# Value loads moved to SP, the activation table loaded first, two weight tiles among the query loads

## Chip, cores and metric

The kernel runs on one core of a Trainium2 chip. The metric is the device time of one execution in microseconds (us). TensorE (PE) multiplies matrices, VectorE (DVE), ScalarE (ACT) and GpSimd (POOL) do elementwise work, SyncE (SP) issues DMAs; ACT can issue DMAs as well.

## What is computed

Attention over 4 batches, 8 heads, 768 positions and head size 64, with a local band (positions closer than 16) joined to 24 block summaries, then layer norm and a two-layer network with a residual:

```python
k_sum = k.reshape(B, H, nb, block, D).max(axis=3)
v_sum = v.reshape(B, H, nb, block, D).mean(axis=3)
scores_l = where(|i - j| < 16, scale * q @ k.T, -1e9)
scores_s = scale * q @ k_sum.T + log(block)
a = softmax(concatenate([scores_l, scores_s]))
attn = a @ concatenate([v, v_sum])
x = heads side by side: (B, S, 512)
xn = (x - mean) / sqrt(var + 1e-6) * g_ln
out = x + maximum(xn @ w_ch1, 0) @ w_ch2        # 512 -> 2048 -> 512
```

The two weight matrices are float64 in memory; the kernel decodes them by integer operations.

## The kernel before

The 3,072 rows are 24 tiles of 128; each tile has two attention steps t of four heads. The first twelve steps (t below 12, the first batch) take an early path in float32: `early_k` copies a window of keys and the block maxima into `kx` (ACT and POOL), `early_qk` multiplies it with the queries `qw` (PE, tile `s`), `softmax` adds the mask and takes the row extreme (DVE, tile `p`) and the exponential (ACT), `early_transp` turns `p` (PE, tile `pp`; ACT copies it to `pT`), `early_pv` multiplies with the values `vw` and with the tail tiles `vst` and `tail` (PE, tile `o`). The block maxima come from four DVE reductions (`kmax`). The block means of the values come from fourteen PE products in `batch_v0` (tile `v`), which need all of the first batch's values; ACT then copies them into the three tail tiles. So no `early_pv` runs ahead of the last value load.

Beside it the weights arrive: `fetch_w(m)` loads a tile of 512 KB (`raw`), `dec_w(m)` decodes it by three DVE instructions and one ACT square, `scale_w` and `conv_w` make two float16 parts of it (`wp`) on ACT and DVE. With them the network's products `g1` (tile `h`) and `g2` (tile `a`) begin; later pairs of tiles use a product scheme of seven multiplications (`sp1`, tiles `qx`, `qy`, `qz`). `warm` gives PE 36 transposes at the start, `spare` is a transpose that fills gaps which the planner foresees on PE.

The order of the work is not written by hand. Every step is recorded by `Plan`, with a cost for each instruction (`cost`, tables `ISSUE`, `LAND`, `SETUP`, `FIRST`), and a list scheduler (`schedule`, called from `search`) makes one list per engine with starting times; `issue` emits the instructions in that order, and each engine runs its list in order. `LOADS` fixes the order of the first loads on SP by hand (`in_front`), ahead of all that the scheduler ranks; `BESIDE` names loads that ACT issues (`queue`): the second half of each of six value tiles. The six calls of `fetch_v0` for a whole tile issue two DMAs of 128 KB each, the seventh one DMA (`vend`, 64 KB). A key tile is 384 KB, a query tile 256 KB, a tail tile two DMAs of 32 KB. Costs of DMAs in the plan: time to issue, bytes by 360 per ns, and a time to landing by kind of step.

Of the kernel before, what the change touches and what calls it, by code (L numbers as in the profile page):

```python
# [18 lines left out]
AF = mybir.ActivationFunctionType  # L19
# [40 lines left out]
RAWS += [f"ring{m}" for m in range(4)]  # L60
AWAY = 24
FILL_IN, FILL_END = 500, 800
LOADS = [("fetch_k0", 0), ("fetch_k0", 1), ("fetch_q", 0), ("gain",), ("fetch_blocks",), ("fetch_k0", 2), ("fetch_k0", 3)]
LOADS += [("fetch_v0", c) for c in range(7)] + [("fetch_tail", 0), ("fetch_q", 1), ("fetch_tail", 1), ("fetch_tail", 2)]
BESIDE = [("fetch_v0", c, 1) for c in range(6)]
NV = 3
HOMES = dict(
    ksg=("qke", "k0_1", "qw4"),
# [30 lines left out]
def in_front(stage, engine):  # L99


    key = (stage[0], *stage[1][:1])
    return LOADS.index(key) if engine == "sync" and key in LOADS else None


class Plan:
# [3 lines left out]
    ENGINES = ("tensor", "vector", "scalar", "gpsimd", "sync")  # L110
    WAIT = dict(tensor=200, vector=140, scalar=160, gpsimd=90, sync=1000)
    SAME = dict(tensor=0, vector=127, scalar=143, gpsimd=100, sync=0)
    SETUP, TICK, SWITCH, FIRST = 1100, 10240 / 3, 93, 3500
    ISSUE = dict(transp=1550, lnT=1250, batch_vput=760, load_q=500)
    LAND = dict(fetch_v0=2050, fetch_k0=1950, fetch_q=2000, fetch_w=1750, fetch_tail=2000, gain=2000)
    LAND |= dict(batch_q=1350, batch_v=1300, load_q=1350, load_v=1150, transp=1050)

    def __init__(self):
# [89 lines left out]
    def cost(self, engine, op, a, k, ins, outs):  # L208

        free = lambda x: math.prod(n for _, n in x.ap[1:])  # L210
        n = max(free(x) for x in ins + outs) if engine != "tensor" else free(a[0])
        if op[:3] == "dma":
            x = (outs + ins)[0]
            return self.ISSUE.get(self.names[self.stage][0], 380 + 70 * (engine == "scalar")), x.ap[0][1] * free(x) * mybir.dt.size(x.dtype) / (200.0 if "transpose" in op else 360.0)
        if engine == "tensor":
            dt = ins[-1].dtype
            if dt == F32R:
                return 0.443 * max(n, 256) + 4.5, 0.0
            if dt == F16 or op == "transpose":
                return max((2 if dt == F32 else 1) * n / 2.4 + 3.0, 28.0), 0.0  # L220
            return max(2 * n / 2.4 + 2.0, 100.0) * 2 if ins[0].ap[0][1] > D else 2 * n / 2.4 + 53.0, 0.0
        psum = any(x.space == bass.MemoryType.PSUM for x in ins)
        pointers = sum(1 for x in ins[1:] if free(x) == 1)
        if engine == "scalar":
            extra = ("accum_out" in k) + sum(isinstance(k.get(x), bass.AP) for x in ("scale", "bias"))
            weights = self.names[self.stage][0] in ("dec_w", "conv_w")
            return n / 1.2 + (51 if psum else 93) + 93 * extra + 35 * weights, 0.0
        if engine == "vector":
            fixed = {"tensor_tensor_reduce": 78, "reciprocal": 90}.get(op, 70) + 61 * pointers
            fixed += 119 * (bool(ins) and self.box(ins[0])[1] == D)  # L230
            return n / (1.92 if op == "tensor_scalar" and not psum else 0.96) + fixed, 0.0
        if op == "tensor_scalar":
            return 180 + n + 61 * pointers + 90 * (n == 1), 0.0
        if op == "tensor_copy":
            return 60 + 3.33 * n, 0.0
        if op == "tensor_tensor":
            shifted = outs[0].offset // outs[0].ap[0][0] != ins[0].offset // ins[0].ap[0][0]
            return 517 if n == 1 else 40 + 2.1 * n + 110 * (shifted or outs[0].dtype == F32R), 0.0
        return 60 + 0.8 * n, 0.0
# [9 lines left out]
    def waits(self, x, real_only=False):  # L249
        wait = []  # L250
        for j, real in x.after.items():
# [3 lines left out]
            else:  # L255
                n = self.names[y.stage][0]
                wait.append((j, (0.0 if real_only else self.slack(x, y)) + (self.LAND.get(n, 1000) if y.dma else self.WAIT[y.engine])))
        return wait
# [157 lines left out]
    def issue(self, nc):  # L416
        for x in self.ops:
            x.first = in_front(self.names[x.stage], x.engine)
        self.watch()
        after = [self.waits(x) for x in self.ops]  # L420
        then = [[] for _ in after]
        for i, x in enumerate(after):
            for j, wait in x:
                then[j].append((i, wait))
        rank = [0.0] * len(after)
        for i in reversed(range(len(after))):
            x = self.ops[i]
            rank[i] = min((rank[j] for j, _ in then[i]), default=0.0) - x.busy - x.moving - self.WAIT[x.engine]
        best = self.search(rank, after, then)
        self.time, self.start, self.end, fills = best  # L430
        for _, i in sorted([*zip(best[1], range(len(after))), *((t, -1) for t in fills)]):
            if i < 0:
                op, a, k = self.ops[self.opens].calls[0]
                getattr(nc.tensor, op)(*a, **k)
                continue
            for op, a, k in self.ops[i].calls:
                getattr(getattr(nc, self.ops[i].engine), op)(*a, **k)  # L437
# [4 lines left out]
def body(ctx: ExitStack, tc, qt, qa, qe, kt, ks, va, vb, vs, g_ln, w1, w2, blocks, out):  # L442
    pl = Plan()
# [8 lines left out]
    def psum(tag, name, shape, at=None):  # L452
        if at is None:
            at = banks[tag] = 1 - banks[tag]
        return pl.tile(pools[tag], shape, F32, f"{tag}{at}", name)
# [12 lines left out]
    wacc = cp.tile([P, 2 * NF], F32, name="wacc")  # L468
# [3 lines left out]
    nc = pl  # L472
# [17 lines left out]
    @pl.step  # L490
    def masks():

        no, far = NEG / QSCALE, nc.gpsimd
        m = msk[:, 1]
        far.memset(m, 0.0)
        for base, a in ((0, 1), (2 * WIN - 2, -1)):
            far.affine_select(m, m, [[a, NC]], compare_op=ALU.is_ge, fill=no, base=base, channel_multiplier=-a)
        far.memset(m[:, P + BLK :], float(np.float32(math.log(BLK)) / np.float32(QSCALE)))
        for t in (0, 2):
            far.tensor_copy(msk[:, t], m)  # L500
        far.memset(msk[:, 0, : WIN - 1], no)
        far.memset(msk[:, 2, P + WIN - 1 : P + BLK], no)

        far.memset(emask[:, :, :D], no)
        far.tensor_copy(emask[:, :, D:], msk[:, :, :P])
        far.tensor_copy(emask[:, :, : NC - P], msk[:, :, P:])
# [28 lines left out]
    def queue(*key):  # L535
        return nc.scalar if any(key[: len(x)] == x for x in BESIDE) else nc.sync

# [103 lines left out]
    @pl.step  # L641
    def batch_s(b):

        mx = work("vm0", f"vm0_{b}", [P, 3])
        nc.vector.tensor_reduce(mx[:], bt["a", b][:], axis=AX.X, op=ALU.max)
        ps = psum("s", f"vps{b}", [P, 512])
        nc.tensor.transpose(ps[:3, :P], mx[:], ident[:])
        m1 = work("vm1", f"vm1_{b}", [3, 8])
        nc.vector.tensor_reduce(m1[:, 0:1], ps[:3, :P], axis=AX.X, op=ALU.max)
        nc.vector.tensor_scalar(m1[:, 0:1], m1[:, 0:1], 2.0**-30, None, ALU.max)  # L650
        mi = m1.bitcast(U32)
        nc.vector.tensor_scalar(mi[:, 1:2], mi[:, 0:1], 0x7F800000, 0x7F800000, ALU.bitwise_and, ALU.bitwise_and)
        nc.vector.tensor_scalar(mi[:, 0:1], mi[:, 1:2], 0x7F800000, 0x7F800000, ALU.bitwise_and, ALU.bitwise_xor)
        nc.vector.tensor_scalar(m1[:, 2:5], ident[:3, :3], m1[:, 0:1], 2.0**13, ALU.mult, ALU.mult)
        nc.vector.tensor_scalar(m1[:, 5:8], ident[:3, :3], m1[:, 1:2], 2.0**-14, ALU.mult, ALU.mult)
        nc.tensor.matmul(ps[:, 128:134], ones[:3], m1[:, 2:8], start=True, stop=True)
        sv = work("sv", f"sv{b}", [P, 10], F32, 2)
        nc.vector.tensor_copy(sv[:, :6], ps[:, 128:134])
        nc.vector.tensor_scalar(sv[:, 6:7], sv[:, 4:5], sv[:, 5:6], QSCALE, ALU.mult, ALU.mult)
        nc.vector.tensor_scalar(sv[:, 7:8], sv[:, 6:7], -1.0, None, ALU.mult)  # L660
        nc.vector.tensor_scalar(sv[:, 8:9], sv[:, 1:2], sv[:, 2:3], None, ALU.mult)
        bt["s", b], bt["c", b] = sv, (sv[:, 7:8], sv[:, 6:7])
# [570 lines left out]
        nc.scalar.activation(gcol[:, 1], gcol[:, 0], AF.Copy, scale=SQ)  # L1233

    @pl.step
    def warm():

        ps = psum("h", "warm", [P, 512])
        with pl.unit():
            for i in range(WARM):  # L1240
                nc.tensor.transpose(ps[:, i % 4 * P : i % 4 * P + P], ident[:], ident[:])
# [40 lines left out]
    def batch(b):  # L1282
# [5 lines left out]
            batch_v(b, c)  # L1288
        batch_s(b)

    warm()
    masks()
    clear()
# [118 lines left out]
```

## Time and profile before

| what | us |
|---|---|
| median of three runs | 615.76 (615.63 to 616.48) |
| profiled execution | 614.82 |
| span of the profiled execution, first to last instruction | 613.0 |
| PE busy in the span | 596.3 (97%) |
| DVE busy in the span | 493.4 (80%) |
| ACT busy in the span | 429.0 (70%) |

Busy time is a mean over stages with different limits, so the views by stretch say more than the table. Instructions of one engine run in the order of its list; idle time before an instruction is put down to what released it last. DMA issues stand in the profile as instructions of the sequencer (SPq, ACTq) and are not counted as busy; nearly every instruction has the line of the planner's emitting loop, so tiles' names tell them apart.

### The profile page before, as it was taken

Reading aid. Unit: us, or ns where it says so; the run is one execution under the profiler, and the core shown is the slowest. Engines: PE = TensorE matmul, PEld = TensorE weight load, DVE = VectorE, ACT = ScalarE, POOL = GpSimd, SP = SyncE. Lnnn points to the kernel's source line nnn. Section 1 sums busy time; section 2 is a strip of 40 time slices with the busy share of each in tenths; the row PEclk is TensorE's granted clock in tenths of the full one; section 3 lists DMA queues with packets and bytes.
Section 4 is the critical chain, followed back from the end, with each engine's and each line's share of the span. In section 5 each row is a group of like instructions: output and inputs, shape, how many; then the busy total and the mean of one; then the engine's idle time right before and its main releaser. Section 6 shows DMA issues by size and latency. Waiting matters only on the chain.

```text
span 613.0 us, 15408 instructions
## 1 busy us (share of the span) xinstructions
PE 596.3 (97%) x5528; PEld 434.0 (71%) x5528; DVE 493.4 (80%) x1260; ACT 429.0 (70%) x1072; POOL 249.0 (41%) x473
## 2 busy tenths in 40 slices
PE   6998899999999999999999999999999999999997
PEld 5586777765677587776866876877777778766675
DVE  3899999999899899999798988889788974633232
ACT  3797798878999977799777857788686575331120
POOL 5122212124675575767664452645445333200000
PEclk9999999999999999999999999999999999999999
DMA  8991388636988977679966757569668461220000
GB/s 250 341 350 31 115 263 279 195 86 138 237 224 203 204 194 181 161 173 220 208 161 150 172 121 152 143 154 198 138 155 180 94 126 45 44 61 18 18 18 35
DMA packets 136237, 95.62 MB, mean 156 GB/s; under 512 B 94561, under 2 KB 118625, under 8 KB 136161
## 3 DMA queue, kind: packets, MB, share of 16 engines
q1 hardware_dynamic: 134528, 93.86, 60.6%
q8 instruction: 43, 0.70, 0.5%
q10 hardware_dynamic: 1632, 0.79, 0.5%
q14 instruction: 34, 0.27, 0.1%
HBM read 66.27 MB, written 6.29 MB: 118 GB/s over the span
## 4 chain that ended last, share of the span: by engine, by line
PE 75%; DVE 13%; DMA 5%; ACT 3%; POOL 2%; issue 1%; SPq 0%; ACTq 0%; POOLq 0%
PE a L437 34%; PE h L437 12%; PE qx L437 10%; PE qz L437 5%; PE s L437 4%; PE o L437 4%; PE qy L437 3%; DVE wf L437 2%; DMA vw<-in_va 1%; DVE raw L437 1%; DVE hl L437 1%; DVE wp L437 1%; PE v L437 1%; DMA ksg<-in_kt 1%; DVE p L437 1%
## 5 line engine op out<-in xcount | busy, mean ns | idle before, releaser
L437 PE MATMUL a<-wp,hh 128*128 128x512 f16 (+1 forms) x768 | 226.6, 377 | 0.0
L437 PEld LDWEIGHTS <-wp 128*128 128x128 f16 x2016 | 163.2, 98 | 25.0 <-issue 2.3
L437 PE MATMUL a<-wp,hl 128*128 128x512 f16 x384 | 144.8, 377 | 0.0
L437 PE MATMUL h<-xs,wp 128*128 128x256 f16 x1152 | 134.1, 273 | 2.2 <-DMA xs<-x 1.0
L437 PEld LDWEIGHTS <-hh 128*128 128x128 f16 x784 | 73.3, 98 | 65.3 <-issue 0.4
L437 POOL TENSOR_TENSOR p<-p,p 128x512 f16<-128x512 f32 x72 | 71.9, 1004 | 35.3 <-ACT p L437 24.5
L437 ACT ACTIVATE p<-p,mn,sv 128x184 f32<-128x184 f32 x144 | 76.1, 530 | 9.1 <-POOL mn L437 8.5
L437 PEld LDWEIGHTS <-hl 128*128 128x128 f16 x392 | 38.3, 98 | 44.6
L437 DVE SCALAR_TENSOR_TENSOR x<-a,wsc,x 128x512 f32<-128x512 f32 (+1 forms) x48 | 35.3, 736 | 22.4 <-PE a L437 22.1
L437 POOL COPY ksg<-ksum 128x48 f32<-128x48 f32 x72 | 29.3, 412 | 52.1 <-DMA ksg<-in_kt 44.8
L437 POOL TENSOR_TENSOR x<-x,rc 128x256 f32<-128x256 f32 x36 | 30.5, 847 | 42.5 <-DVE x L437 31.7
L437 POOL TENSOR_SCALAR mn<-mn,sv 128x2 f32<-128x2 f32 x72 | 31.1, 434 | 40.4 <-DVE mn L437 37.6
L437 DVE CUSTOM_DVE_ANT_0 p<-s,mask 128x184 f32<-128x184 f32 x144 | 42.7, 337 | 3.6 <-PE s L437 3.6
L437 PE MATMUL qx<-xs,wp 128*128 128x128 f16 x576 | 38.4, 219 | 0.0
L437 PEld LDWEIGHTS <-wd 128*128 128x128 f16 x576 | 33.8, 98 | 3.1
L437 DVE SCALAR_TENSOR_TENSOR kl<-ksg,sv,kh 128x368 f16<-128x368 f32 x48 | 34.2, 721 | 1.5 <-ACT kh L437 1.2
L437 ACT ACTIVATE kh<-ksg,sv 128x368 f16<-128x368 f32 x48 | 28.5, 594 | 9.4 <-PE s L437 3.4
L437 DVE SCALAR_TENSOR_TENSOR hl<-h,hh 128x512 f16<-128x512 f32 x48 | 32.3, 678 | 2.0 <-ACT hh L437 1.8
L437 ACT CAST p<-p 128x512 f16<-128x512 f32 x72 | 33.3, 505 | 0.2
L437 ACT ACTIVATE v<-vst,sv 128x512 f16<-128x512 f32 x36 | 25.7, 716 | 9.2 <-PE o L437 7.8
L437 DVE SCALAR_TENSOR_TENSOR v<-vst,sv,v 128x512 f16<-128x512 f32 x36 | 30.2, 838 | 1.3 <-ACT v L437 1.1
L437 ACT ACTIVATE hh<-h 128x512 f16<-128x512 f32 x48 | 28.0, 584 | 4.4 <-PE h L437 4.3
(209 smaller groups left out, 1217.0 us busy)
## 6 DMA issues: line engine op xcount, KB each, us to landing
raw<-in_w SPq DMA_DIRECT2D x32, 512.0 KB
ksg<-in_kt SPq DMA_DIRECT2D x72, 184.0 KB
out_x<-x SPq DMA_DIRECT2D x23, 256.0 KB
qw<-in_qt SPq DMA_DIRECT2D x36, 128.0 KB
vst<-in_va SPq DMA_DIRECT2D x36, 128.0 KB
qs<-in_qt SPq DMA_DIRECT2D x36, 128.0 KB
vst<-in_vb SPq DMA_DIRECT2D x80, 32.0 KB
bst<-in_ks SPq DMA_DIRECT2D x12, 192.0 KB
```

Source lines behind the costliest of these rows:

```text
L437: getattr(getattr(nc, self.ops[i].engine), op)(*a, **k)
```

## The change

Four things change. The second halves of the value tiles, which ACT issued (`BESIDE`), are issued by SP like the first halves. A new step `table`, ranked first on DVE and ACT, clears one column and takes its exponential, so that the activation table is loaded before anything else on ACT. In the fixed order of loads on SP, `gain` (the layer norm's gains, `gcol`) goes from fourth place behind the four key loads, and the first two weight tiles get places of their own: behind the first tail tile, and behind the second. And the costs in the plan are altered: the DMA rings begin at 1300 instead of 3500, the issue of several first loads and of the transposes in `split1` and `split2` is set to its own value, some loads get a rate of their own, weight tiles land after 1550 instead of 1750, `gain` after 3000 instead of 2000.

```diff
-LOADS = [("fetch_k0", 0), ("fetch_k0", 1), ("fetch_q", 0), ("gain",), ("fetch_blocks",), ("fetch_k0", 2), ("fetch_k0", 3)]
-LOADS += [("fetch_v0", c) for c in range(7)] + [("fetch_tail", 0), ("fetch_q", 1), ("fetch_tail", 1), ("fetch_tail", 2)]
-BESIDE = [("fetch_v0", c, 1) for c in range(6)]
+LOADS = [("fetch_k0", 0), ("fetch_k0", 1), ("fetch_q", 0), ("fetch_blocks",), ("fetch_k0", 2), ("fetch_k0", 3), ("gain",)]
+LOADS += [("fetch_v0", c) for c in range(7)] + [("fetch_tail", 0), ("fetch_w", 0), ("fetch_q", 1), ("fetch_tail", 1)]
+LOADS += [("fetch_w", 1), ("fetch_tail", 2)]
+BESIDE = []
...
+    if stage[0] == "table":
+        return 0
...
-    SETUP, TICK, SWITCH, FIRST = 1100, 10240 / 3, 93, 3500
-    ISSUE = dict(transp=1550, lnT=1250, batch_vput=760, load_q=500)
-    LAND = dict(fetch_v0=2050, fetch_k0=1950, fetch_q=2000, fetch_w=1750, fetch_tail=2000, gain=2000)
+    SETUP, TICK, SWITCH, FIRST = 1100, 10240 / 3, 93, 1300
+    ISSUE = dict(transp=1550, lnT=1250, split1=1250, split2=1250, batch_vput=760, load_q=500)
+    ISSUE |= dict(fetch_v0=650, fetch_tail=430, fetch_q=420, fetch_k0=430, gain=430)
+    RATE = dict(fetch_v0=300.0, fetch_w=410.0, fetch_q=385.0)
+    LAND = dict(fetch_v0=2050, fetch_k0=1950, fetch_q=2000, fetch_w=1550, fetch_tail=2000, gain=3000)
...
+    def table():
+        nc.vector.memset(wacc[:, :1], 0.0)
+        nc.scalar.activation(wacc[:, :1], wacc[:, :1], AF.Exp)
...
+    table()
     warm()
```

In `cost`, the bytes of a DMA are divided by the step's `RATE`, where it has one, and by 360 where not.

## Rows read from the trace of the kernel before

**Rows 1.** Busy time by stretch: the stretch and its length in us, busy us and instructions (x) of PE, PE's weight loads, DVE, ACT and POOL, granted share of the TensorE clock, DMA share, GB/s.

```profile
0.00:8.50 8.50, 6.91 (x37) 6.76 (x37) 2.12 (x8) 0.28 (x1) 7.00 (x44) 1.00 0.82 243
8.50:18.90 10.40, 6.84 (x29) 3.63 (x29) 4.03 (x19) 6.29 (x19) 1.60 (x9) 0.84 0.97 296
18.90:80.00 61.10, 55.48 (x450) 45.30 (x449) 58.90 (x182) 51.66 (x143) 12.93 (x36) 1.00 0.60 201
80.00:613.00 533.00, 527.07 (x5017) 378.36 (x5014) 428.32 (x1055) 370.73 (x913) 227.44 (x384) 1.00 0.61 147
```

**Rows 2.** The chain of work that ended last, in order of time, pieces of the first 60 us: start, us, what.

```profile
20.47 3.81 PE v L437 x8
...
40.25 0.69 DVE xs L437
```

**Rows 3.** Busy time of the instructions on the tile `spare` alone (the fillers), by stretch: the stretch and its length, busy us and instructions (x) of PE and of PE's weight loads, granted clock, DMA share, GB/s.

```profile
40.00:60.00 20.00, 5.55 (x46) 5.07 (x46) 1.00 0.35 98
60.00:80.00 20.00, 1.12 (x7) 0.91 (x7) 1.00 0.41 129
```

**Rows 4.** Timeline of DVE up to 19.2 us: start, us, what, and idle time before it with its releaser.

```profile
3.91 0.95 DVE L437 TENSOR_REDUCE kmax<-k 128x24 f32<-128x768 f32 x1 [2.91 <-DMA k<-in_ks]
...
11.01 0.36 DVE L437 CUSTOM_DVE_ANT_0 p<-s,emask 128x192 f32<-128x192 f32 x1 [4.40 <-PE s L437]
...
17.78 0.36 DVE L437 CUSTOM_DVE_ANT_0 p<-s,emask 128x192 f32<-128x192 f32 x1 [3.86 <-PE s L437]
...
18.88 0.42 DVE L437 TENSOR_SCALAR wf<-raw 128x512 uint32<-128x512 uint32 x1
```

**Rows 5.** Timeline of SP's issues up to 20 us: start, us, what.

```profile
0.72 0.87 SPq L437 DMA_DIRECT2D k<-in_ks  x2
1.64 0.64 SPq L437 DMA_DIRECT2D qw<-in_qe  x1
2.32 0.62 SPq L437 DMA_DIRECT2D gcol<-in_g_ln  x1
3.90 0.34 SPq L437 DMA_DIRECT2D blk<-in_blocks  x1
...
8.03 3.94 SPq L437 DMA_DIRECT2D vw<-in_va  x6
...
12.66 0.41 SPq L437 DMA_DIRECT2D qw<-in_qe  x1
```

**Rows 6.** SP's own waits, first from 0 to 13 us and then from 16.5 to 19 us: who waited for what, us in total, times, longest; and the issue that the last of them held.

```profile
SPq L437 <- DMA k<-in_ks: 2.3, 2, 1.4
SPq L437 <- DMA qw<-in_qe: 1.3, 1, 1.3
...
SPq L437 <- DVE mn L437: 0.6, 1, 0.6
SPq L437 <- DMA vw<-in_va: 0.3, 1, 0.3
...
SPq L437 <- DMA raw<-in_w: 0.7, 1, 0.7
...
17.80 0.31 SPq L437 DMA_DIRECT2D tail<-in_vb  x1
```

**Rows 7.** Timeline of ACT up to 10 us.

```profile
0.89 7.25 ACTq L437 DMA_DIRECT2D vw<-in_va  x6
8.22 1.28 ACT L437 ACT_TABLE_LOAD   x1 [8.22 <-DMA vw<-in_va]
9.52 0.52 ACT L437 COPY kx<-k 128x158 f32<-128x158 f32 x2
```

**Rows 8.** Timeline of PE up to 24.3 us.

```profile
8.32 0.27 PE L437 MATMUL s<-ident 128*128 128x128 f32 x1
9.94 0.91 PE L437 MATMUL s<-kx,qw 64*128 64x184 f32 x8 [1.35 <-issue]
...
20.40 2.84 PE L437 MATMUL v<-vw,blk 128*120 128x512 f32 x6
23.17 1.11 PE L437 MATMUL v<-vend,blk 32*120 32x512 f32 x2
```

**Rows 9.** Busy time by stretch as in Rows 1, for three other stretches.

```profile
2.00:8.50 6.50, 6.50 (x37) 6.35 (x35) 1.91 (x2) 0.28 (x1) 5.57 (x34) 1.00 1.04 313
...
13.70:18.90 5.20, 5.17 (x16) 2.54 (x17) 1.34 (x10) 1.98 (x7) 0.70 (x4) 0.67 0.99 312
...
20.00:40.00 20.00, 19.40 (x147) 14.97 (x146) 19.21 (x73) 18.57 (x53) 3.31 (x14) 1.00 1.00 369
```

**Rows 10.** DVE's waits from 18.9 to 80 us: who waited for whom, us in total, times, longest.

```profile
DVE wsc L437 <- POOL wsc L437: 0.7, 1, 0.7
DVE xn L437 <- POOL rs L437: 0.4, 1, 0.4
DVE p L437 <- ACT pT L437: 0.4, 1, 0.4
DVE p L437 <- PE s L437: 0.2, 1, 0.2
```

**Rows 11.** SP's instructions that transpose into the tile `xs` late in the span: count, ns min/median/max, first and last start.

```profile
L437 SPq DMA_TRANSPOSE xs<-x_a x6: 1231/1234/1577, 303.6 to 529.4; - x6
```

**Rows 12.** Timeline of the last microseconds: the last instruction of DVE, with its wait for PE's last.

```profile
609.93 0.48 DVE L437 SCALAR_TENSOR_TENSOR x<-last,wsc,x 128x256 f32<-128x256 f32 x1 [0.17 <-PE last L437]
```

More of the change, by code (lines that the diff above doesn't have):

```diff
@@ L213, in cost @@
             x = (outs + ins)[0]
-            return self.ISSUE.get(self.names[self.stage][0], 380 + 70 * (engine == "scalar")), x.ap[0][1] * free(x) * mybir.dt.size(x.dtype) / (200.0 if "transpose" in op else 360.0)
+            return self.ISSUE.get(self.names[self.stage][0], 380 + 70 * (engine == "scalar")), x.ap[0][1] * free(x) * mybir.dt.size(x.dtype) / (200.0 if "transpose" in op else self.RATE.get(self.names[self.stage][0], 360.0))
         if engine == "tensor":
@@ L1235, in warm @@
     @pl.step
+    def table():
+        nc.vector.memset(wacc[:, :1], 0.0)
+        nc.scalar.activation(wacc[:, :1], wacc[:, :1], AF.Exp)
+    @pl.step
     def warm():
```

## Prediction

> **What bounds the kernel now.** I read the busy times by stretch first. From 80 us on PE works 527.07 of 533 us [rows 1]; what is missing is mostly the last stores. So the end of the kernel is PE's work plus whatever PE wastes before 80 us, and a change at the start counts only as far as it takes such waste away. Between 18.9 and 80 us PE is busy 55.48 of 61.1 us, and of that time 5.55 + 1.12 = 6.7 us went into fillers [rows 3]: together 5.6 + 6.7 = 12.3 us of waste. In the same stretch DVE is busy 58.90 of 61.1 us [rows 1]: DVE decodes the weights, and until it has, PE lacks work. The chain of waits says the same with a finer grain: values and PE up to 24 us, a float32 attention chain until 40 us, then DVE [rows 2]. DVE is full from the first decoding instruction on, at 18.88 us [rows 4]. Before that it is busy 2.12 + 4.03 = 6.2 of 18.9 us [rows 1]. So the question of this change is: **at what time does DVE become full?** Each us earlier there is worth up to one us at the end, as long as the 12.3 us of PE's waste last.
>
> What held the first decoding? The weight tile had landed at 17.80 us: that landing released SP's next issue [rows 6]. DVE, in the order of its list, had four mask instructions of the second attention step ahead, and they began at 17.78 us, when PE had made their scores [rows 4]. So 1.1 us is the list's, and the rest is the DMA's.
>
> **The change part by part.** *Table.* ACT loads its table for 1.28 us, behind 7.25 us of DMA issues, and copies the first keys at 9.52 us [rows 7]. Now the table comes at about 1 us, with a memset and an exponential of one column, below 0.3 us each by the nearest small instruction (the 0.27 us of a transpose [rows 8]), and queued behind that exponential's wait for the memset are only the key copies: cost 0, hidden by the wait for the first keys (until 3.91 us [rows 4]). The first score product can't come at 6 us for all that: `warm` and a transpose keep PE until 8.32 + 0.27 = 8.59 us. So it comes at 8.6 instead of 9.94 us [rows 8], 1.35 us earlier. By itself this ends at no one who is late: DVE's mask instructions move from 11.01 us, but the decoding does not wait for those.
>
> *Order on PE.* The second step's scores and the value means come from a plan in which loads land nearer to the truth. From 8.6 us PE has two score products (0.91 each), twelve transposes (at most 0.27 each, 3.2) and fourteen mean products (2.84 for six, 1.11 for the last two [rows 8], so 6.8 in all), 11.8 us: done by about 20.4 us, where they ended at 24.28. The scores need less than 2 us of this and need not wait for values, so the first steps' masks can lie before 17 us and no longer hold the decoding: **1.1 us of DVE**. The attention chain is some 4 us ahead, which should also end DVE's waits for it later on: 0.4 + 0.2 = **0.6 us** [rows 10]. The other 1.1 us of DVE's waits there are for POOL's powers and stay.
>
> *Value loads on SP.* Six more issues at 3.94 / 6 = 0.66 us [rows 5] are 3.9 us on SP ahead of the first weight tile. On the other side, SP waited 2.3 + 1.3 + 0.6 + 0.3 = 4.5 us in that time for landings [rows 6], while ACT's loads shared the DMA engines. Without any wait the first weight tile is issued at 0.72 + 13.0 us: twelve value loads 7.9, four key loads 1.7, a query tile 0.64, `blk` 0.34, `gcol` 0.62, `vend` as one of the value loads 0.66, two tail loads 1.2 (as `gcol`; [rows 5]). A load that has the engines to itself takes 3.91 - 0.72 = 3.2 us from issue to use for 384 KB [rows 4, 5]; 512 KB at 312 GB/s [rows 9] add 0.4. That is 13.7 + 3.6 = 17.3 us. By bytes: ahead of the end of that tile lie 256 KB less (the second query tile) and 64 KB more (the tail), 192 KB at 312 GB/s = 0.6 us: 17.80 - 0.6 = 17.2 us. I take 17.2, so **0.6 us earlier**. The bounds: all 4.5 us of SP's waits remain (18.2 + 3.6 = 21.8 us, 4 us later); or the engines reach the 369 GB/s of the stretch from 20 us on [rows 9] instead of 312, which would bring the bytes some 2 us forward, while the issue lets the tile come no earlier than 17.3. So the lower end is 17.2 too. I stay there, as the engines were already full in this stretch, at 1.04 and 0.99 [rows 9].
>
> Here a rule of the Trainium skill bears on it: "DMA: Bandwidth & Descriptors", section "Issuing engines are not separate DMA queues", holds that issuing from several engines saves only the sequencer's time, which is usually small beside the DMA. In this trace it is not small: an issue every 0.66 us [rows 5] against 128 KB at 313 GB/s, 0.42 us [rows 9]. By the rule the tile lands at 17.2 whatever SP does; by the row SP is as late as the bytes are.
>
> *Second weight tile, queries.* The second query tile and a tail tile now come between the weight tiles: 256 + 64 + 512 KB after the first, 852 kB at 312 GB/s, 2.7 us, so at 19.9 us. DVE is through with the first at 17.2 + 1.8 (0.42 and two of 0.7 us) = 19.0 us. What lies between are the masks of the third step, whose queries come 0.8 us after the tile, at 18 us, and whose scores take another 0.91 [rows 8]: about 1 us of DVE's work for a hole of 0.9. Either the scores come in time (0) or they wait behind a value product (0.9); I charge the middle, **0.4 us**.
>
> *gain* goes behind the keys: its one user, ACT's square after the first decoding, is not due before 17 us; cost 0, and 1 us of that square if it were as late as 18. *Costs in the plan* add no instruction. They re-order everything, the late stages too: the transposes of `split1` and `split2` do take 1.23 us [rows 11] and were planned at 0.38, while SP has room there. Bounds for the new order after 80 us: PE waits 5.9 us now, some 3 of them from PE's last product at 609.8 us to the end of the last store at 613.0 [rows 1, 12]; the other 2.9 may go (-2.9) or double (+2.9). I take 0 as neither has a reason.
>
> **Sum.** 1.1 + 0.6 + 0.6 - 0.4 = 1.9 us. On the profiled execution: span 613.0 - 1.9 = 611.1, with the 1.8 us around it 612.9; it lay 0.94 us below the median of the runs, so the median goes from 615.76 to **613.9**.
>
> **Rivals.** *More of DVE's holes close.* All 2.2 us of DVE's idle time from 18.9 to 80 us go with the attention chain ahead, and no hole comes: 1.1 + 0.6 + 2.2 = 3.9 us: 611.9. For it: ACT gets 7 us back, and PE's half speed is gone (a granted 0.67 between 13.7 and 18.9 us [rows 9], a mix of 1.2 and 2.4 GHz, after PE had idled for 1.35 us and more). Against it: half of that idle time is POOL's.
>
> *Given back later.* The head gains what I say, but the re-made list has new waits of about 2 us behind 80 us, where now there are 2.9: about 615.7. For it: the chain there passes from engine to engine with little to spare, and every list of the scheduler is new. Against it: PE's queue has enough work there that 500 us pass with next to no wait.
>
> *SP becomes the bound (slower).* Each load on SP waits until an earlier one has landed, as now for the keys and queries. If the 4.5 us of waits stay, the first weight tile lands at 21.8 us and DVE is full 21.8 - 18.88 = 2.9 us later; less the 0.6 us of holes, +2.3: 618.1. It decides from the point where SP's waits exceed 1.6 us (17.3 + 1.6 = 18.9). For it: 0.66 us an issue is more than a transfer. Against it: just because of that, the landings catch up with the issues, and ACT's loads no longer lie between.
>
> *The change does not do it.* If `warm` and the values still hold PE until 24 us and the list still puts the masks ahead of the decoding, only the 0.6 us of bytes remain: 615.2.
>
> **How the numbers follow.** Forecast 0.48 (612.6 to 614.6 by itself), more holes closed 0.13, given back or not done 0.24, SP bound 0.15. A measurement of this kernel can tell about 0.2%, 1.2 us, from no change: faster than 614.5 has 0.13 and nearly all of the 0.48: 0.60; within it 0.25; slower 0.15. The range reaches over the second and third case and leaves out SP's: 611.4 to 616.9.
>
> **What would show it.** In the profile after: the table load within the first 3 us; first score product at about 8.6 us; last value product before 21 us; first decoding instruction at about 17.2 us, and DVE full from there; fewer fillers or less idle PE before 80 us by about 2 us; PE's idle time behind 80 us near 5.9 us. Wrong at the first step if the decoding begins at 18.9 or later; wrong in the pass-through if it begins early and PE's time after 80 us begins no earlier.

## The result, and the profile after

The kernel after takes 620.24 us (median of 6 runs, 618.76 to 622.01) beside 615.69 us before (6 runs): a ratio of 1.0073, 95% interval 1.0052 to 1.0094. It is slower by 4.5 us where 1.9 us of gain were forecast, and outside the range. The profiled execution took 620.18 us with a span of 618.4 us, 5.4 us above the 613.0 us of before.

The kernel after, busy time by stretch, columns as in [rows 1]:

```profile
0.00:8.50 8.50, 6.80 (x37) 6.76 (x37) 3.17 (x11) 2.44 (x6) 7.11 (x43) 1.00 0.80 256
8.50:18.90 10.40, 10.25 (x47) 5.08 (x46) 4.38 (x19) 5.97 (x18) 1.46 (x11) 1.00 0.90 251
18.90:80.00 61.10, 52.63 (x421) 45.41 (x420) 54.75 (x170) 47.05 (x133) 12.21 (x33) 0.94 0.56 197
80.00:618.40 538.40, 531.36 (x5051) 381.99 (x5049) 433.81 (x1064) 374.89 (x919) 225.58 (x387) 1.00 0.62 146
```

The head did improve: up to 18.9 us PE works 17.05 us instead of 13.75, and at full clock. The loss is in the third row, the very stretch in which DVE was to be full: DVE is busy 54.75 us instead of 58.90, PE 52.63 instead of 55.48, at a granted clock of 0.94 instead of 1.00. What PE has not done by 80 us stands in the fourth row: 4.3 us more work, 531.36 instead of 527.07 us.

The fillers in the kernel after, columns as in [rows 3]. They take 9.87 us in this stretch; before it was 5.55 + 1.12, and none ahead of 40 us:

```profile
18.90:40.00 21.10, 2.17 (x19) 2.19 (x20) 1.00 1.01 384
40.00:60.00 20.00, 5.03 (x45) 4.66 (x43) 0.88 0.27 84
60.00:80.00 20.00, 2.68 (x13) 2.05 (x13) 0.95 0.37 113
```

**The books of PE**, in microseconds of useful work at full clock. Busy time at half clock counts half. In the kernel after PE was busy 6.65 us between 55.13 and 61.96 us, of which 0.94 us were fillers and are counted in their own row; in the kernel before it was busy 3.42 us between 14.07 and 17.49 us, without fillers. Both stretches have a granted 0.50 (kernel after first, columns as in [rows 1]):

```profile
55.13:61.96 6.83, 6.65 (x30) 5.66 (x31) 4.99 (x19) 5.31 (x15) 0.94 (x4) 0.50 0.06 19
...
14.07:17.49 3.42, 3.42 (x12) 1.54 (x11) 0.00 (x0) 0.80 (x2) 0.12 (x1) 0.50 0.98 323
```

| | before | after | worse by |
|---|---|---|---|
| idle up to 18.9 us | 5.15 | 1.85 | -3.3 |
| idle 18.9 to 80 us | 5.62 | 8.47 | 2.85 |
| fillers | 6.67 | 9.87 | 3.2 |
| lost to half clock, without fillers | 1.71 | 2.86 | 1.15 |
| idle behind 80 us | 5.93 | 7.04 | 1.1 |

The sum is 5.0 us, against the spans' 5.4. So nearly the whole loss of this execution is placed. The head gives PE 3.3 us of idle time and the 1.7 us that its half clock cost before, 5.0 us. The stretch behind it takes 2.85 + 3.2 + 2.86 = 8.9 us, and the rest of the kernel 1.1.

The row on the clock compares two executions, not the two kernels. The profiled execution of the kernel before has a mean granted clock of 0.997, that of the kernel after 0.994. Over the 24 to 31 runs of the kernel before that were made beside each experiment the mean is 0.993 to 0.994, and over the six runs of the kernel after it is 0.994. So, as far as six runs can tell, the amount of half clock does not set the kernel after apart from the kernel before, though it stands in these books. Where in the kernel it falls, and what it costs there, is seen only in the profiled executions.

What held each engine there? SP's issues, ACT's and PE's starts and DVE's decoding in the kernel after (timelines; start, us, what, idle time and its releaser), to be read against [rows 4, 5, 7, 8]:

```profile
4.01 8.28 SPq L442 DMA_DIRECT2D vw<-in_va  x12
...
13.93 0.42 SPq L442 DMA_DIRECT2D raw<-in_w  x1
14.40 0.42 SPq L442 DMA_DIRECT2D qw<-in_qe  x1
14.92 0.85 SPq L442 DMA_DIRECT2D vst<-in_vb  x2
15.82 0.43 SPq L442 DMA_DIRECT2D raw<-in_w  x1
```
```profile
0.71 1.28 ACT L442 ACT_TABLE_LOAD   x1 [0.71 <-PEq L1413]
...
3.95 0.32 ACT L442 COPY kx<-k 128x158 f32<-128x158 f32 x1 [1.75 <-DMA k<-in_ks]
```
```profile
8.62 0.91 PE L442 MATMUL s<-kx,qw 64*128 64x184 f32 x8
...
16.50 1.11 PE L442 MATMUL v<-vend,blk 32*120 32x512 f32 x2
```
```profile
13.79 0.08 DVE L442 DVE_READ_ACCUMULATOR2_ANT mn<- 128x1 f32 x1
17.73 0.43 DVE L442 TENSOR_SCALAR wf<-raw 128x512 uint32<-128x512 uint32 x1 [3.86 <-DMA raw<-in_w]
18.19 0.69 DVE L442 SCALAR_TENSOR_TENSOR wf<-raw,wf 128x512 uint32<-128x512 uint32 x1
18.92 0.69 DVE L442 SCALAR_TENSOR_TENSOR raw<-raw,wf 128x512 uint32<-128x512 uint32 x1
21.11 0.43 DVE L442 TENSOR_SCALAR wf<-raw 128x512 uint32<-128x512 uint32 x1 [1.50 <-DMA raw<-in_w]
```

The table and the scores are where the prediction put them, the values are through earlier, and the first decoding comes at 17.73 us, 0.5 us later than forecast and 1.15 us earlier than before. But 1.9 us later DVE is empty again: the second weight tile, issued behind a query tile and a tail, lands 3.4 us after the first one was taken up.

DVE's waits from 18.9 to 80 us in the kernel after, to be read against [rows 10], where they made 1.7 of the 2.2 us in which DVE was idle:

```profile
DVE kmax L442 <- DMA bst<-in_ks: 1.8, 1, 1.8
DVE wf L442 <- DMA raw<-in_w: 1.5, 1, 1.5
DVE p L442 <- PE s L442: 1.3, 1, 1.3
DVE xn L442 <- POOL rs L442: 0.7, 1, 0.7
DVE rc L442 <- PE o L442: 0.6, 1, 0.6
DVE wsc L442 <- POOL wsc L442: 0.4, 1, 0.4
```

And the pieces of its chain that answer to [rows 2] (start, us, what): landings of weight tiles stand in it up to 41 us, where PE's values and the attention chain stood, and a landing of 4.5 us from 66 us on, where DVE's own work stood.

```profile
15.82 5.26 DMA raw<-in_w
...
22.18 10.21 DMA raw<-in_w
32.40 8.96 DMA raw<-in_w
...
66.26 4.53 DMA bst<-in_ks
```

The clock fell after a pause of PE (its timeline in the kernel after). The eight products with `kx`, 0.91 us at 2.4 GHz, take 1.62 us here; DVE's waits of 1.3 and 0.6 us for `s` and `o`, at 59.3 and 60.8 us, lie in this stretch.

```profile
52.09 0.96 PE L439 MATMUL spare<-ident 128*128 128x128 f32 x7
54.17 0.78 PE L442 MATMUL pp<-ident,p 128*128 128x128 f32 x3 [1.11 <-ACT p L442]
55.20 0.90 PE L442 MATMUL pp<-ident,p 128*128 128x128 f32 x3 [0.25 <-ACT p L442]
...
57.69 1.62 PE L442 MATMUL s<-kx,qw 64*128 64x184 f32 x8
```

### The profile page after: what moved, and what is told of

It is laid out like the page before. It is cut to its first block, busy times and chain, and to the rows that moved or that the text cites. A ratio compares the mean times of both kernels' runs of the same rounds, so it can differ in the third digit from the quotient of the medians.

```text
span 618.4 us, 15469 instructions
## 1 busy us (share of the span) xinstructions
PE 601.0 (97%) x5549; PEld 439.2 (71%) x5549; DVE 496.1 (80%) x1261; ACT 430.4 (70%) x1073; POOL 246.4 (40%) x473
## 4 chain that ended last, share of the span: by engine, by line
PE 77%; DMA 9%; DVE 8%; ACT 2%; issue 1%; SPq 1%; POOL 1%; POOLq 0%; ACTq 0%; DVEq 0%
PE a L442 36%; PE h L442 14%; PE qx L442 10%; PE qz L442 5%; PE s L442 4%; DMA raw<-in_w 4%; PE o L442 4%; PE qy L442 2%; DMA bst<-in_vs 2%; DVE wf L442 2%; DVE raw L442 1%; PE warm L442 1%; DVE hl L442 1%; DMA bst<-in_qa 1%; DMA ksg<-in_kt 1%
## 5 line engine op out<-in xcount | busy, mean ns | idle before, releaser
L442 PE MATMUL a<-wp,hl 128*128 128x512 f16 (+1 forms) x384 | 144.7, 377 | 0.0
L442 POOL TENSOR_SCALAR mn<-mn,sv 128x2 f32<-128x2 f32 x72 | 34.0, 474 | 54.4 <-DVE mn L442 54.2
L442 POOL COPY ksg<-ksum 128x48 f32<-128x48 f32 x72 | 25.0, 350 | 39.5 <-DMA ksg<-in_kt 36.4
L442 PE MATMUL qx<-xs,wp 128*128 128x128 f16 x576 | 36.7, 219 | 0.0
```

## The experiments

Three theories. **The head**: what the diff says it does costs time by itself (SP late, the load order, the table). **The costs**: with the new numbers the scheduler makes lists that are systematically worse. **The draw**, a lottery: every re-made set of lists has waits of its own, for either set of numbers; this one drew badly. Later, for this one set of lists: **the hole** at the second weight tile, or **the clock**.

All ratios are to the kernel before, run beside each kernel on the same chip.

### The change with the lists held

Here each engine keeps the list of the kernel before. The search's result is split into one queue for each engine, parts of the change are then made by hand, and the queues are merged again along the dependencies:

```diff
-        for _, i in sorted([*zip(best[1], range(len(after))), *((t, -1) for t in fills)]):
+        if MOVED:
+            for x in self.ops:
+                if x.dma and x.engine == "scalar":
+                    x.engine = "sync"
...
+            queues.setdefault(e, []).append((place[i] - 1e9 if i in place else t, i))
...
+        if TABLE:
+            nc.vector.memset(self.wacc[:, :1], 0.0)
+            nc.scalar.activation(self.wacc[:, :1], self.wacc[:, :1], AF.Exp)
+        for i in line:
```

**held_sp**: value loads on SP and the table first, SP's first loads in the old order.

```diff
+NEWLOADS = list(LOADS)
+MOVED, TABLE = True, True
```

> The lists of the kernel before, planned with its own costs, are kept on all engines; only the table is loaded first and the six value loads of ACT go to SP, in the old order of loads. Theory List (the head gains what was forecast, and the loss is made by the re-made list): the head gains and nothing is made anew, so 0 to 2.5 us below the kernel before; with the old order of the masks ahead of the decoding, about 1 us. Theory Loads (SP alone is too late with the weights): the first weight tile lands later than 17.8 us and the time is 1 us or more above.

Measured: 618.03 us, 1.0034 (1.0012 to 1.0056). **held_all**: the new order of loads as well.

```diff
+NEWLOADS += [("fetch_v0", c) for c in range(7)] + [("fetch_tail", 0), ("fetch_w", 0), ("fetch_q", 1), ("fetch_tail", 1)]
+NEWLOADS += [("fetch_w", 1), ("fetch_tail", 2)]
+MOVED, TABLE = True, True
```

> As the one above, and the first loads on SP stand in the order of the kernel after (gain behind the keys, the first two weight tiles among queries and tails). All other engines keep the lists of the kernel before. Theory List: 0 to 2.5 us below the kernel before. Theory Loads: the second weight tile comes at 21 us as in the kernel after, DVE has a hole of about 1.5 us, and the time is 1 to 4 us above.

Measured: 620.10 us, 1.0048 (1.0030 to 1.0065). Neither is the change alone. In held_sp the old order puts the weight tiles behind the tails; in held_all the list of DVE wants weight tile 1 first, and the load order brings tile 0 first. First decoding in the timelines of DVE, held_sp and then held_all:

```profile
20.70 0.43 DVE L478 TENSOR_SCALAR wf<-raw 128x512 uint32<-128x512 uint32 x1 [5.23 <-DMA raw<-in_w]
```
```profile
21.45 0.43 DVE L480 TENSOR_SCALAR wf<-raw 128x512 uint32<-128x512 uint32 x1 [4.49 <-DMA raw<-in_w]
```

So they price a late weight tile, the mechanism of the rival that SP becomes the bound: 1.8 and 2.6 us later than before, 2.1 and 3.0 us at the end (the ratios by 616 us). A part of that may be the clock's: over their runs the mean granted clock is 0.993 and 0.992, beside 0.994 in the kernel before. Two versions without these slips, and the table by itself:

**held_sp2**: ACT's value loads each directly behind their siblings on SP and the table first, nothing else re-placed.

```diff
+NEWLOADS = []
...
+                    mate = next(j for j, y in enumerate(self.ops) if y.stage == x.stage and y.dma and y is not x)
+                    best[1][self.ops.index(x)] = best[1][mate] + 0.01
```

> The lists of the kernel before on every engine, SP's too; the six value loads of ACT stand on SP behind their siblings, and the table is loaded first. In the first pair of kernels with held lists the first weight tile came behind all the tails, or second where DVE's list wants it first; here the order on SP is that of the kernel before. Theory SP late: six more issues (3.9 us) come ahead of the first weight tile, whose issue moves from 13.1 to 14 us or later; DVE's first decoding begins at 18.9 or up to 20 us, 0 to 1.5 us above the kernel before. Theory Head gains: issue without waits at 13.7 us or before, first decoding below 18 us, 1 us or more below the kernel before.

**held_all2**: held_all with the two weight tiles exchanged in the load order, so that the one which the list decodes first comes first.

```diff
-NEWLOADS += [("fetch_v0", c) for c in range(7)] + [("fetch_tail", 0), ("fetch_w", 0), ("fetch_q", 1), ("fetch_tail", 1)]
-NEWLOADS += [("fetch_w", 1), ("fetch_tail", 2)]
+NEWLOADS += [("fetch_v0", c) for c in range(7)] + [("fetch_tail", 0), ("fetch_w", 1), ("fetch_q", 1), ("fetch_tail", 1)]
+NEWLOADS += [("fetch_w", 0), ("fetch_tail", 2)]
```

> As the one above, with the first loads on SP in the order of the kernel after, and of the two weight tiles that one first which DVE's list decodes first. Theory SP late: 0 to 1.5 us above the kernel before. Theory Head gains: first decoding at 17.7 us as in the kernel after, second at 21 us, net 0 to 1.5 us below.

**held_table**: the table alone.

```diff
+NEWLOADS = []
+MOVED, TABLE = False, True
```

> The kernel before with its lists; only the table comes first on ACT, ahead of ACT's six value loads, which stay there. ACT's copies of the keys come at about 8.3 instead of 9.52 us and the first scores at 8.7 instead of 9.94. Theory Head gains: the masks of the second step come earlier by about 1 us and so does the decoding, 0.5 to 1 us below the kernel before. Theory SP late says nothing on it; if the first scores lie beside what counts, within 0.5 us.

Measured, in this order: 616.15 us, 1.0017 (0.9986 to 1.0048); 616.95 us, 1.0015 (0.9987 to 1.0042); 615.16 us, 0.9989 (0.9963 to 1.0016). First decoding in the timelines of DVE:

```profile
17.86 0.43 DVE L480 TENSOR_SCALAR wf<-raw 128x512 uint32<-128x512 uint32 x1 [2.17 <-DMA raw<-in_w]
...
18.01 0.43 DVE L480 TENSOR_SCALAR wf<-raw 128x512 uint32<-128x512 uint32 x1 [0.76 <-DMA raw<-in_w]
...
18.23 0.42 DVE L478 TENSOR_SCALAR wf<-raw 128x512 uint32<-128x512 uint32 x1
```

The decoding starts 0.65 to 1.0 us earlier than before, and nothing of that can be told at the end. DVE has lost it again by 80 us: up to there it has been busy 63.3, 64.4 and 65.1 us, in the kernel before 65.05. The clock doesn't hide a gain either: over their runs its mean is 0.994, 0.994 and 0.995, beside 0.994 in the kernel before. In held_all2 the hole before the second weight tile is there too (0.93 us at 20.82), the term that the prediction charged with 0.4. So the change of the head, with the work behind it in its old order, lies by the intervals of the first two between 0.14% faster and 0.48% slower: the head is not what cost 4.5 us (0.73%), and it doesn't bring 1.9 (0.31%).

### Costs and loads apart

**costs_only**: the new numbers in the plan, loads, engines and steps as before.

```diff
-    SETUP, TICK, SWITCH, FIRST = 1100, 10240 / 3, 93, 3500
+    SETUP, TICK, SWITCH, FIRST = 1100, 10240 / 3, 93, 1300
...
+    RATE = dict(fetch_v0=300.0, fetch_w=410.0, fetch_q=385.0)
```

> Loads, engines and steps of the kernel before; only the costs in the plan are those of the kernel after, so that the lists are made anew. Theory List: the time moves by 2 us or more either way although nothing that is executed has changed but its order, and more likely up, as in the kernel after. Theory Loads: within 1 us of the kernel before.

**loads_only**: the kernel after with the old numbers.

```diff
-    SETUP, TICK, SWITCH, FIRST = 1100, 10240 / 3, 93, 1300
+    SETUP, TICK, SWITCH, FIRST = 1100, 10240 / 3, 93, 3500
...
-    RATE = dict(fetch_v0=300.0, fetch_w=410.0, fetch_q=385.0)
```

> Table, loads on SP and their order as in the kernel after, planned with the costs of the kernel before, so that the lists are made anew too. Theory Loads: as slow as the kernel after, 3 to 5 us above the kernel before. Theory List: this is another list, and its time is its own, anywhere from 2 us below to 5 us above; the head shows the same 1 us of earlier decoding or less.

Measured: 621.60 us, 1.0077 (1.0047 to 1.0107), and 618.01 us, 1.0021 (1.0005 to 1.0036). A loss as large comes with the numbers alone, without any of the changed loads, and not by the clock, whose mean over the runs of costs_only is 0.995. By these two, the costs are bad, or the draw is.

### Other draws

The search varies priorities with seeded random numbers. Other seeds give other lists for the same program and the same numbers. Of the six starts of the search the first was undisturbed; here it is disturbed as well:

```diff
-            rnd = random.Random(s)
-            tried = [r + rnd.uniform(-NOISE, NOISE) * (s > 0) for r in rank]
+            rnd = random.Random(s + 100)
+            tried = [r + rnd.uniform(-NOISE, NOISE) for r in rank]
```

The four kernels are before and after with 100 and with 200.

> The kernel before, planned with other random numbers (100 added to the seeds, all six starts disturbed): another list of the same work by the same costs. Theory Lottery (each list has its own time, and the kernel before had a good draw): 616 to 622 us, as far off as the kernel after. Theory Costs (the new costs make worse lists): within 1.5 us of the kernel before.

> As the one above, another draw (200 added). Theory Lottery: its own time, 616 to 622 us, and not that of the other draw. Theory Costs: within 1.5 us of the kernel before.

> The kernel after with 100 added to the seeds. Theory Lottery: anywhere from 613 to 622 us, and one of the two draws below 617. Theory Costs: 618 to 622 us like the kernel after, in both draws.

> The kernel after with 200 added to the seeds. Theory Lottery: anywhere from 613 to 622 us. Theory Costs: 618 to 622 us.

| lists | program and numbers before | program and numbers after |
|---|---|---|
| as given | 1 | 1.0073 (1.0052 to 1.0094) |
| + 100 | 1.0065 (1.0030 to 1.0099) | 1.0015 (0.9996 to 1.0034) |
| + 200 | 1.0020 (0.9996 to 1.0043) | 1.0002 (0.9979 to 1.0025) |

The medians were 620.27, 618.62, 618.24 and 616.13 us. The theory of the costs falls: with other seeds the new numbers give lists as good as the kernel before, and the old numbers one that is nearly as bad as the kernel after. The mean of each column is 1.003. Three draws each are few; they show a scatter of 0.7% in either column, not that the columns have the same mean.

### PE kept busy in the head

**before_fill**: more transposes of the identity on PE ahead of the first two sets of `early_transp`.

```diff
+FILLS = {("early_transp", 0, 0): 11, ("early_transp", 0, 1): 6, ("early_qk", 0): 0}
...
+                for _ in range(FILLS.get((n, *a), 0)):
+                    op, a, k = x.calls[0]
+                    nc.tensor.transpose(a[0], self.ident[:], self.ident[:])
```

> The kernel before, with 11 and 6 more transposes of the identity on PE ahead of the first two sets of transposes of p, where PE idles 1.41 and 0.80 us before its clock falls to 1.2 GHz from 14.1 to 17.5 us. Their results are overwritten. Theory Clock: the clock stays at 2.4 GHz, the value products and the second scores take half, the decoding begins about 1 us earlier, and the time falls by 0.5 to 1.5 us. If the clock there does not count: within 0.3 us, or up by what the fillers take.

Measured: 615.77 us, 0.9986 (0.9955 to 1.0016). The list does the second of the two steps first, so the 6 came ahead of the 11, and the clock fell all the same, from 11.86 to 15.28 us. It leaves the question of the clock in the head open.

### What in this set of lists costs the time

**after_w01**: the kernel after with its own lists held; on SP the second weight tile comes directly behind the first.

```diff
+NEWLOADS = [x for x in LOADS if x[0] != "fetch_w"]
+NEWLOADS[NEWLOADS.index(("fetch_q", 1)) : NEWLOADS.index(("fetch_q", 1))] = [("fetch_w", 0), ("fetch_w", 1)]
+MOVED, TABLE = False, False
```

> The lists of the kernel after, held; on SP alone the second weight tile comes directly behind the first, ahead of the second query tile and the tails. Hole theory (the 1.5 us that DVE idles at 21.1 us for the second weight tile are carried to the end): that hole is closed, and the median is 1.5 us below the kernel after's 620.2, so 618.7, 1.005 of the kernel before. Clock theory (the end is late since PE fell to 1.2 GHz from 55.1 to 62.0 us): no gain by itself, 1.007, unless the earlier decoding also closes the 1.1 us that PE idles at 54.2 us. Theory that nothing local decides (many small waits of a new order): between 1.005 and 1.009, with the hole gone and the 1.5 us lost again before 80 us.

**after_fill**: the kernel after with more transposes where PE paused at 54.2 us.

```diff
+FILLS = {("early_transp", 6, 0): 9, ("early_transp", 6, 1): 2}
```

> The kernel after with 9 and 2 more transposes of the identity on PE ahead of two transposes of the attention step that it reaches at 54.2 us, to fill the 1.1 us in which PE waited there for ACT. They compute nothing that is used. Clock theory: PE stays at 2.4 GHz behind it, the 3.4 us that 6.9 us at half speed cost are kept as far as nothing else is late, and the median falls by 1.5 to 3.4 us, to 617 to 618.7 (1.002 to 1.005 of the kernel before). Hole theory and the theory that nothing local decides: the clock may stay up, but the time is that of the kernel after within 1 us (619.2 to 621.2), as DVE and the waits for transfers at 70 us set the pace.

**after_w01_fill**: both edits.

> Both edits together. If hole and clock are the cause and add up: 1.5 + 1.5 to 3.4 us below the kernel after, 615.3 to 617.2, about 1.000 of the kernel before. If only one counts, that one's time. If neither counts: 619 to 621, 1.006 to 1.008.

| | us | ratio |
|---|---|---|
| after_w01 | 619.95 | 1.0069 (1.0045 to 1.0093) |
| after_fill | 619.38 | 1.0050 (1.0028 to 1.0072) |
| after_w01_fill | 617.02 | 1.0024 (1.0007 to 1.0041) |

Alone, neither can be told from the kernel after. Together they take back some 3 of the 4.5 us (1.0024 instead of 1.0073), and that interval lies wholly below the kernel after's. Busy time by stretch of after_w01_fill:

```profile
18.90:80.00 61.10, 55.45 (x456) 47.02 (x456) 58.24 (x176) 50.32 (x141) 13.30 (x36) 0.97 0.59 210
80.00:614.80 534.80, 528.08 (x5027) 379.83 (x5024) 430.11 (x1058) 372.85 (x911) 226.72 (x384) 1.00 0.59 146
```

DVE is busy 58.24 us in the stretch and PE 55.45, as in the kernel before (58.90 and 55.48), and 3.3 us less is left for later than in the kernel after. The books of PE close here too: idle 1.9 + 5.65, fillers 9.61 and 1.58 for the added transposes, 1.5 lost at half clock (62.02 to 65.44 us, a filler of 0.42 us apart), idle 6.72 at the end make 26.9 us, against 25.1 in the kernel before; the spans differ by 1.8.

What does each edit leave? In after_w01 the hole is gone, but the pause ahead of the 54 us mark stays (1.12 us), and a later wait grows to the full: PE's product `tx` needs `xn`, which stands on DVE behind the `kmax` that waits for `bst`. PE's timeline in after_w01, and then its stretch of half clock:

```profile
68.29 0.27 PE L481 MATMUL spare<-ident 128*128 128x128 f32 x1
71.66 0.66 PE L484 MATMUL tx<-ident,xn 128*128 128x128 f32 x2 [3.10 <-DVE xn L484]
```
```profile
70.85:77.68 6.83, 6.02 (x29) 5.05 (x30) 6.67 (x21) 4.44 (x14) 1.65 (x5) 0.50 0.30 90
```

The fall of the clock has moved there, as long as it was. In after_fill the clock does fall less, for 3.4 us from 64.07 us on, but the holes at the weight tiles are still on DVE, larger than in the kernel after (stretch of half clock, then DVE's timeline):

```profile
64.07:67.48 3.41, 3.41 (x18) 2.81 (x18) 3.13 (x9) 3.33 (x15) 0.00 (x0) 0.50 0.66 183
```
```profile
22.01 0.43 DVE L449 TENSOR_SCALAR wf<-raw 128x512 uint32<-128x512 uint32 x1 [1.82 <-DMA raw<-in_w]
...
25.09 0.43 DVE L449 TENSOR_SCALAR wf<-raw 128x512 uint32<-128x512 uint32 x1 [0.76 <-DMA raw<-in_w]
```

With both, the wait for `bst` shrinks from 1.8 to 1.0 us (1.3 in after_fill), PE has no pause above 0.85 us from 18.9 to 80 us, and half clock lasts 3.4 us instead of 6.8, as in after_fill.

That the two edits together take back some 3 us is measured. That they are worth more together than the sum of both is not shown: the ratios of the two alone lie 0.0004 and 0.0023 below the kernel after's, the ratio of both 0.0049, and each interval is some 0.002 either way. How they do it is read from one profiled execution of each. And it is not all a mending of what the new lists lost: over their runs the mean granted clock is 0.9937 in the kernel after, 0.9942 in after_w01, 0.9961 in after_fill and 0.9965 with both, but 0.993 in the kernel before beside them. By an estimate from these means, (0.9965 - 0.9937) x 617, up to 1.7 of the 3 us are a clock that is better than that of the kernel before, and after_w01_fill is the slower one even so.

**table_fill**: the lists of before held, the table first, and PE kept busy ahead of the first scores and transposes.

```diff
+NEWLOADS = []
+MOVED, TABLE = False, True
+FILLS = {("early_qk", 0): 9, ("early_transp", 0, 1): 11, ("early_transp", 0, 0): 6}
```

> The kernel before with its lists held, ACT's table loaded first, and 9, 11 and 6 more transposes of the identity on PE ahead of the first scores and of the first two sets of transposes, to keep PE busy between 9 and 19 us. They compute nothing that is used. If a head with PE at 2.4 GHz and scores 1 us earlier passes its gain on: 1 to 2 us below the kernel before, 613.8 to 614.8 (0.997 to 0.998). If the head is given back, as the held lists have shown so far: 1.000 within 0.002.

Measured: 615.18 us, 0.9990 (0.9975 to 1.0004): not to be told from the kernel before. PE is at full clock until 71 us and busy 17.08 us up to 18.9 us, 3.3 us more than before; the added transposes take 1.15 + 1.42 + 0.82 = 3.4 us of that, so what the head gains is the clock, and half clock now comes from 71.68 to 75.09 us. That gain is given back too, though over its runs the mean granted clock is 0.997, beside 0.993 in the kernel before. None of the 16 kernels beats the kernel before by more than its interval.

## Why the prediction was wrong

**Right: what the edits do at the head.** Table in the first 2 us, first scores at 8.62 (8.6 forecast), the last value product ended at 17.61 (before 21), the masks of the second step no longer in front of the decoding. SP issued the first weight tile at 13.93 us (13.7 without any wait): its waits did not stay, and the rival of SP as the bound did not come about, though a late tile does cost what it was priced at, or nearly so (held_sp, held_all). The first decoding came at 17.73 instead of 17.2 us: 1.15 us of the two terms 1.1 + 0.6. From its issue to its use the tile took 3.8 us, not 3.6; the 3.2 us for a key load, on which the 3.6 rest, were read as those of a load that has the engines to itself, but ACT issued value loads beside it from 0.89 us on [rows 7].

**Too small: the hole at the second weight tile.** Charged with 0.4 us as the middle of 0 and 0.9; it measured 1.50 us. The tile landed at about 21.1 us where 19.9 was forecast from bytes, and the masks of the third step, which were to lie between, came at 22.18 us.

**The step that failed: "Costs in the plan add no instruction. They re-order everything ... I take 0 as neither has a reason."** Two things were wrong in it. Its bounds were set at 2.9 us either way from PE's idle time *behind* 80 us; there the new order did cost 1.1. But the stretch before, 18.9 to 80 us, was re-ordered as well, and was taken as full "from there" once DVE had begun. There PE lost 8.9 us of useful time in the profiled execution: 2.85 idle, 3.2 more in fillers, 2.86 at half clock. The head had given it 5.0. Of these the half clock is a loss beside this one execution of the kernel before; over its other runs that kernel has as much of it. And zero was not the fair middle: the kernel before has the lowest of the six medians in the table of draws, as ratios. With loads_only and costs_only there are seven other sets of lists, of either numbers, 0.02 to 0.77% above it, 0.39% in the mean, or 2.4 us. With that in place of 0, which could not be known before, the sum would have been 615.76 - 1.9 + 2.4 = 616.3 us, which is no change. The other 4 us are, by the same numbers, 2.1 us by which this draw lies above that mean, as one of the two slowest of the seven, and the 1.9 us that did not reach the end.

**The pass-through failed too.** "Each us earlier there is worth up to one us at the end": in held_sp2, held_all2 and held_table DVE began 0.65 to 1.0 us earlier, was no further by 80 us (by its busy time), and no gain showed at the end. DVE was not full from its first decoding on. Of the 0.6 us of waits that were to close, DVE's wait for `pT` is gone; but in the kernel after it waits 6.3 us in all, where only POOL's 1.1 us are those of before.

**The nearest rival** was "given back later". Its mechanism, new waits of the re-made list, was the right one, but it put them behind 80 us and priced them at about 2 us, which is what the head was to gain; nothing in the mechanism sets that as its limit.

What stays open: the 1.1 us (by medians) or 1.5 us (by the ratio) between after_w01_fill and the kernel before, which of the new waits cost how much, why the kernel before is the fastest of its eight sets of lists, and whether the new numbers, over many draws, give better or worse lists than the old.

## What to carry to other kernels

A change that makes a list scheduler run again is two changes: hold the old lists and make the edit alone to learn what the edit is worth, and draw a few lists with other seeds to learn what a list is worth, before either is believed. Here all seven re-made sets lay above the lists of the kernel before, four of them by more than their interval, and a gain of a head below the scatter of the draws (here 0.7%) can't be forecast from the head alone. Two mends that can't be told from nothing one by one may show together, here 3 us. And before a stretch at half clock in one profiled execution is called a loss, compare the mean granted clock over all runs of both kernels: here they were the same.

## What was not expected of the hardware

A pause of PE of 1.11 us up to 54.17 us, with 0.25 us more at 55.20, was followed by 6.8 us at 1.2 GHz; in after_w01 3.10 us up to 71.66 were, and 1.12 us up to 53.95 were not. In after_w01_fill 3.4 us at 1.2 GHz came at 62.02 us with no pause above 0.85 us since 18.9 us. How much of a run PE spends at 1.2 GHz differs from run to run of the same kernel. In the kernel after the time follows it: the six runs have spans of 616.9 us (twice) at a mean granted clock of 0.997, 618.4 and 618.5 at 0.994, 619.0 at 0.992 and 620.1 at 0.988. Elsewhere it need not: held_table took 613.53 us at 0.994 and 619.08 us at 0.997. Over its runs the mean of the kernel after is 0.994, that of the kernel before 0.993 to 0.994; in after_w01_fill, 12 runs, 0.9965; in after_s200, 10 runs, 0.998, and in its profiled execution the clock does not fall at all between 6.6 us and the last microsecond.

An issue on SP is not priced by bytes alone: twelve loads of 128 KB into `vw` take 8.28 us, 0.69 us each, and a load of 512 KB into `raw` 0.42 us.
